# Decay attention and two feed-forward stages on one core: blocks rebuilt at an even pace, weight casts spaced out, sums kept in PSUM, and a minimum by a one-tensor operation

## The chip, the core and the metric

The kernel runs on one core of a Trainium2 chip. The metric is the device time of one execution in microseconds (us), the median of three runs. One execution was also profiled; all rows below come from it.

## What is computed

```python
scores = (q @ k^T) / 8 + (cum[i] - cum[j])      # cum = cumsum(log(clip(f, 1e-4, 1))), causal
attn = softmax(scores);  x = attn @ v           # 4 batches, 8 heads, 576 rows, 64 columns
h = x @ w_in;   x = (h * clip(h + 3, 0, 6) / 6) @ w_out       # 2304 tokens, 512 -> 2048 -> 512
h = x @ w_in2;  out = (max(h, 0) + alpha * min(h, 0)) @ w_out2  # alpha per column of h
```

Inputs are fp32; the weights come as 64-bit floats that the kernel itself turns into fp32. Every fp32 product is made of three fp32r products: high by high, high by low, low by high.

## The kernel before

The whole program is one hand-written order of instructions for each engine (a manual schedule); nothing reorders it later.

**Attention** works on 16 pairs of heads, 9 units a pair: four blocks of 128 rows of head a, a tail unit with the last 64 rows of both heads, four blocks of head b. A unit passes through stages that lag one another by a few units: PE makes scores (L364 to L381), DVE row maxima (`maxes`, L341; the tail unit has two columns of maxima, whose smaller one L343 keeps, both negated), ACT the exponentials with row sums (L349), PE the transposes (L397), ACT or DVE their copies (L408, L413). Per pair follow the reciprocals of the row sums (`recips`, L420 to L424), the product with v (L454) and its scaling into `r` (L461). `prep_head` and `prep_low` split the q and k of one head into high and low parts (POOL L92, POOL L332, DVE L333); two rows of sums of logarithms ride along as extra rows of k, taken from DRAM scratch `aq_d` and `ak_d` (L313, L314). The program's beginning builds these rows: `ak` on DVE, `aq` on POOL, then DMAs to scratch.

**Side work** stands in tables of name and unit. `CONV_ATT` gives the unit at which each step of the conversion of the first weights is issued: `m`, `f`, `s`, `j`, `g` turn raw words into fp32 (ACT L137, DVE L140, L144, L148, L153), `S1` to `S4` add or subtract weight blocks (POOL L167), `h` and `l` cast to high and take the low part (ACT L181, POOL L185). `fetch` loads raw weights. `CONV_TURN` is such a table for the start of the second feed-forward stage, in slots after the set at which it is started.

**The feed-forward stages** are 48 sets (stage, group of 256 columns of h, block of 768 tokens). A set has seven products (`product`, L700, six matmuls each) that form four blocks of h from seven sums of blocks, in PSUM banks hA (two), hB and hC. Between the products stand the pieces of the set before: L731 in the first stage, L733 in the second, which multiply by w_out. After a product, `keep` copies it (ACT L705) or `add` adds it to a kept copy (DVE L708), and `activate` follows: L663 (first stage) or L666 and L668 (second) on ACT, then DVE L674 or L677, then ACT's high copy L682 and POOL's low part L683, which the pieces need. The queue `later` sets what must follow, `aside` puts side work behind it in the slot. `build` rebuilds the input blocks of the next token block: 8 adds (L237), 14 casts to high (ACT L240), 14 low parts (L245). For two of them the places come from `BUILD`, for others from `BUILD_FIRST` at an even rate.

Of the kernel before, what the change touches and what calls it, by code (L numbers as in the profile page):

```python
# [21 lines left out]
def decay_attention_ffn2_kernel(ctx, tc, qk, v, f, wi1, wo1, wi2, wo2, alpha, out):  # L22
    nc = tc.nc
# [22 lines left out]
    CONV_ATT = "m0 15 f0 16 s0 17 j0 18 g0 19 m1 24 f1 25 s1 26 j1 27 g1 28 hb 33 lb 35 S1 42 S3 42 S2 44 S4 44 ha 51 la 53 hc 53 lc 60 hd 60 ld 62 m2 69 f2 70 s2 71 j2 72 g2 73 m3 78 f3 79 s3 80 j3 81 g3 82 ho0 78 lo0 80 ho1 87 lo1 89 wi0 90 wi1 93 wo0 99 wo1 102"  # L46
# [231 lines left out]
    def attention():  # L278
        with ExitStack() as ax:
# [57 lines left out]
            def maxes(parts, dsts):  # L337
# [4 lines left out]
                if n == 2:  # L342
                    nc.vector.tensor_tensor(out=nm[:, 0:1], in0=nm[:, 0:1], in1=nm[:, 1:2], op=ALU.min)  # L343
# [153 lines left out]
            nc.sync.dma_start(out=alpha_sb, in_=alpha)  # L497
            aug_consts(0)
# [5 lines left out]
            nc.gpsimd.memset(aq.bitcast(F32)[:, :, 512:640], 0.0)  # L504
            nc.gpsimd.memset(aq.bitcast(F32)[:, 2:4, 0:512], -1.0)
# [44 lines left out]
            aside(2, lambda: fetch(0), lambda: fetch(1))  # L550
# [103 lines left out]
    def activate(s, gt, i, n, h, d):  # L654
# [5 lines left out]
        def first():  # L660
# [28 lines left out]
    def product(s, c, gt, k):  # L689
# [17 lines left out]
        def add(k2):  # L707
            nc.vector.tensor_add(out=c[k2], in0=h, in1=c[k2])  # L708
# [194 lines left out]
```

## Time and profile before

| quantity | value |
|---|---|
| runs | 1013.59, 1015.56, 1016.53 us; median 1015.56 |
| profiled execution | 1012.13 us, of which the span of the instructions is 1010.3 |
| mean granted clock of PE | 0.995 of full speed |
| PE busy | 965.5 us, 96% of the span |
| DVE busy | 735.9 us, 73% |
| ACT busy | 589.1 us, 58% |
| POOL busy | 590.0 us, 58% |
| bytes moved by DMA | 147.57 MB |

An engine is busy in the time of its computing instructions. PE is TensorE, DVE VectorE, ACT ScalarE, POOL GpSimd, SP the engine whose queue issues most DMAs. In a timeline, the brackets at a row's end give the idle time ahead of it and what ended it.

### The profile page before, as it was taken

What the parts mean: (1) busy time and instruction counts of PE and PEld (TensorE: products, weight loads), DVE (VectorE), ACT (ScalarE), POOL (GpSimd) and SP (SyncE); (2) the same over time, 40 slices, a digit from 0 to 9 for tenths busy, and PEclk for the clock granted to TensorE, in tenths of its full rate; (3) what the DMA queues carried; (4) which work ended last, traced back from release to release, by engine and by line L of the source; (5) the groups of instructions that cost most, each with busy time, mean ns of one, the idle gap of its engine ahead of it and who ended that gap; (6) DMA issues with size and microseconds to landing.
All of it is one profiled execution on the core that took longest, in us unless ns stands there. A gap on an engine that the chain in (4) does not pass through costs nothing.

```text
span 1010.3 us, 15919 instructions
## 1 busy us (share of the span) xinstructions
PE 965.5 (96%) x5488; PEld 859.7 (85%) x5488; DVE 735.9 (73%) x1284; ACT 589.1 (58%) x1444; POOL 590.0 (58%) x577
## 2 busy tenths in 40 slices
PE   4999999999999999999999989999999999999998
PEld 3767666678899999998998988789898888898997
DVE  6888988857698788878989846145687788735454
ACT  5677787776555555555654445665565656564452
POOL 8567568956646666566485269566556556532222
PEclk9999999999999999999999999999999999999999
DMA  6555576501424444310576851332344420243531
GB/s 219 174 173 168 176 239 208 150 2 42 156 66 177 178 175 169 107 48 1 198 308 241 308 184 48 137 129 81 125 160 168 166 84 1 104 182 142 229 150 68
DMA packets 36868, 147.57 MB, mean 146 GB/s; under 512 B 4668, under 2 KB 4668, under 8 KB 33652
## 3 DMA queue, kind: packets, MB, share of 16 engines
q1 hardware_dynamic: 36784, 146.56, 41.7%
q8 instruction: 43, 0.70, 0.3%
q14 instruction: 37, 0.30, 0.1%
q10 hardware_dynamic: 4, 0.00, 0.0%
HBM read 98.26 MB, written 44.14 MB: 141 GB/s over the span
## 4 chain that ended last, share of the span: by engine, by line
PE 57%; DVE 23%; POOL 7%; ACT 6%; issue 4%; DMA 2%; SPq 0%; POOLq 0%; ACTq 0%; DVEq 0%
PE o L733 13%; PE hA L700 12%; PE o L731 12%; PE hC L700 7%; PE pv L454 4%; PE hB L700 3%; DVE nm L341 3%; PE tp L397 2%; DVE t L674 2%; PE sc L364 2%; POOL wi L185 2%; POOL g L683 1%; DVE r L751 1%; DVE s L708 1%; ACT g L682 1%
## 5 line engine op out<-in xcount | busy, mean ns | idle before, releaser
L731 PE MATMUL o<-g,wo 128*128 128x384 f32 x1152 | 233.3, 341 | 2.0 <-POOL g L683 2.0
L700 PE MATMUL hA<-xh,wi 128*128 128x384 f32 x768 | 225.8, 339 | 9.0 <-ACT s L705 5.4
L733 PE MATMUL o<-wo,g 128*128 128x512 f32 x864 | 225.5, 395 | 4.0 <-POOL g L683 3.0
L683 POOL TENSOR_TENSOR g<-t,g 128x384 fp32r<-128x384 f32 x120 | 128.8, 1073 | 156.1 <-ACT g L682 134.6
L731 PEld LDWEIGHTS o<-g,wo 128*128 128x128 f32 x1152 | 205.6, 189 | 4.6 <-POOL g L683 3.3
L733 PEld LDWEIGHTS o<-wo,g 128*128 128x128 f32 x864 | 159.8, 188 | 33.2 <-POOL g L683 6.2
L683 POOL TENSOR_TENSOR g<-s,g 128x384 fp32r<-128x384 f32 x72 | 74.7, 1038 | 155.6 <-ACT g L682 153.8
L700 PEld LDWEIGHTS hA<-xh,wi 128*128 128x128 f32 x768 | 142.0, 188 | 15.1 <-ACT s L705 7.6
L751 DVE TENSOR_TENSOR r<-o,r 128x512 f32<-128x512 f32 x126 | 86.2, 687 | 73.8 <-PE o L733 73.7
L700 PE MATMUL hA<-xl,wi 128*128 128x384 f32 x384 | 129.7, 338 | 0.0
L682 ACT CAST g<-t 128x384 fp32r<-128x384 f32 x120 | 61.9, 515 | 113.0 <-DVE t L674 97.3
L700 PE MATMUL hC<-xh,wi 128*128 128x384 f32 x384 | 115.0, 340 | 3.6 <-ACT s L705 3.6
L740 DVE SCALAR_TENSOR_TENSOR r<-o,r 128x384 f32<-128x384 f32 x168 | 90.6, 549 | 21.2 <-PE o L731 21.0
L349 ACT ACTIVATE p<-sc,nm 128x128 f32<-128x128 f32 (+4 forms) x160 | 84.6, 532 | 22.9 <-DVE nm L341 10.9
L245 POOL TENSOR_TENSOR xl<-r,xh 128x384 fp32r<-128x384 f32 x65 | 78.5, 1225 | 4.1 <-ACT xh L240 3.7
L341 DVE TENSOR_REDUCE nm<-sc 128x1 f32<-128x128 f32 (+4 forms) x160 | 71.7, 470 | 10.1 <-PE sc L366 8.5
L700 PEld LDWEIGHTS hC<-xh,wi 128*128 128x128 f32 x384 | 71.3, 189 | 6.7 <-ACT s L705 4.6
L700 PEld LDWEIGHTS hA<-xl,wi 128*128 128x128 f32 x384 | 72.4, 189 | 3.1
L682 ACT CAST g<-s 128x384 fp32r<-128x384 f32 x72 | 37.1, 515 | 60.1 <-DVE s L677 53.4
L397 PE MATMUL tp<-ident,p 128*128 128x128 f32 x384 | 68.6, 282 | 0.6 <-ACT pt L413 0.6
L364 PE MATMUL sc<-k,q 128*128 128x256 f32 (+2 forms) x128 | 55.6, 434 | 11.9 <-DVE k L332 9.8
L700 PE MATMUL hC<-xl,wi 128*128 128x384 f32 x192 | 65.1, 339 | 0.0
(128 smaller groups left out, 1901.8 us busy)
## 6 DMA issues: line engine op xcount, KB each, us to landing
wid<-wi SPq DMA_DIRECT2D x24, 896.0 KB
wi<-wid SPq DMA_DIRECT2D x12, 1792.0 KB
rqk<-in_qk SPq DMA_DIRECT2D x32, 608.0 KB
raw<-in_wi SPq DMA_DIRECT2D x32, 512.0 KB
raw<-in_wo SPq DMA_DIRECT2D x32, 512.0 KB
wod<-wo SPq DMA_DIRECT2D x24, 512.0 KB
wo<-wod SPq DMA_DIRECT2D x12, 1024.0 KB
vt<-in_v SPq DMA_DIRECT2D x16, 320.0 KB
```

What stands on the lines that cost most here:

```text
L245: e.tensor_sub(out=XS[k][1][:, b, c], in0=x, in1=XS[k][0][:, b, c].bitcast(F32))
L341: nc.vector.tensor_reduce(out=nm[:, i:i + 1], in_=src, axis=AX.X, op=ALU.max, negate=True)
L349: nc.scalar.activation(out=pt[:, c0:c0 + cw], in_=src, func=AF.Exp, bias=nm[:, 0:1], scale=1.0, accum_out=dsts[i])
L364: nc.tensor.matmul(out=sc[:, 0:n], lhsT=q1[:, qs], rhs=k1[:, 0:n], start=True, stop=False)
L397: nc.tensor.transpose(tp[:, j, :], pt[:, 128 * j:128 * j + 128], ident)
L682: nc.scalar.copy(out=gt[n][i][:, 0], in_=hold["g"])
L683: nc.gpsimd.tensor_sub(out=gt[n][i][:, 1], in0=hold["g"], in1=gt[n][i][:, 0].bitcast(F32))
L700: nc.tensor.matmul(out=h, lhsT=a, rhs=b[:, x, kc], start=new and kc + e == 0, stop=kc == KH - 1 and e == 2, skip_group_check=not new)
L731: nc.tensor.matmul(out=o[:, 0:NB], lhsT=a[:, cs], rhs=b, start=st, stop=sp)
L733: nc.tensor.matmul(out=o, lhsT=b[:, cs], rhs=a, start=st, stop=sp)
L740: later(0, lambda: nc.vector.scalar_tensor_tensor(out=acc, in0=o[:, 0:NB], scalar=1.0 / 6.0, in1=acc, op0=ALU.mult, op1=ALU.add))
L751: nc.vector.tensor_add(out=acc, in0=o, in1=acc)
```

## The change

It has seven parts. (1) The minimum L343 becomes a tensor_scalar with the second column as the scalar. (2) The scratch rows `aq_d` are written by DMA straight from `ak` and from constants, without POOL's copies; the preparation of head 1 moves behind the masks on POOL. (3) The first two raw weight loads and the conversions that use them move to later units. (4) `CONV_TURN` gets other slots. (5) All rebuilds take their places from one list, at an even rate that depends on the rebuild; in two of them the eight adds move from DVE to POOL and the low parts are shared out evenly. (6) `add` leaves its sum in the PSUM bank, except for product 7. (7) The second stage's activation is written as h + (1 - alpha) * relu(-h), without the second Relu.

```diff
-    CONV_ATT = "m0 15 f0 16 s0 17 j0 18 g0 19 m1 24 f1 25 s1 26 j1 27 g1 28 hb 33 lb 35 S1 42 S3 42 S2 44 S4 44 ha 51 la 53 hc 53 lc 60 hd 60 ld 62 m2 69 f2 70 s2 71 j2 72 g2 73 m3 78 f3 79 s3 80 j3 81 g3 82 ho0 78 lo0 80 ho1 87 lo1 89 wi0 90 wi1 93 wo0 99 wo1 102"
+    CONV_ATT = "m0 20 f0 21 s0 22 j0 23 g0 24 m1 26 f1 27 s1 28 j1 29 g1 30 hb 34 lb 35 S1 42 S3 42 S2 44 S4 44 ha 51 la 53 hc 53 lc 60 hd 60 ld 62 m2 69 f2 70 s2 71 j2 72 g2 73 m3 78 f3 79 s3 80 j3 81 g3 82 ho0 78 lo0 80 ho1 87 lo1 89 wi0 90 wi1 93 wo0 99 wo1 102"
...
-    CONV_TURN = "p0 0 p1 0 S1 6 S2 7 S3 7 hc 8 ha 8 lc 9 hb 9 la 10 lb 11 S4 12 hd 13 ld 14 p2 14 p3 15 ho0 24 lo0 25 ho1 26 lo1 27 wi0 40 wi1 43 wo0 46 wo1 48"
-    BUILD_FIRST = "h0 l0 a3 h3 l3 h2 l2 a4 a6 h6 l6 h4 l4 h1 l1 a5 h5 l5"
-    BUILD = "h0 2 l0 4 a3 6 h3 9 l3 11 h2 9 l2 11 a4 13 a6 15 h4 16 l4 18 h1 17 l1 19 h6 19 l6 21 a5 22 h5 26 l5 28"
+    CONV_TURN = "p0 0 p1 0 S1 5 S2 6 S3 7 hc 9.5 ha 10.5 lc 10.6 la 11.5 hb 12 lb 13 S4 14 hd 17 ld 18 p2 15 p3 18.5 ho0 24 lo0 25 ho1 26 lo1 27 wi0 40 wi1 43 wo0 46 wo1 48"
+    BUILD_FIRST = "h0 l0 a3 a4 h3 h2 l2 l3 a6 h4 l4 h1 h6 l1 a5 l6 h5 l5"
...
-    def build_ops(k, p, add, subs, even=None):
+    def build_ops(k, p, add, subs, even):
         adds, highs, lows = build_parts(k, p, add, subs)
-        if even is not None:
...
-        return [(t, {"h": highs, "l": lows, "a": adds}[name[0]][int(name[1]), c])
-                for name, t in table(BUILD) for c in range(KH)]
+        fns = [{"h": highs, "l": lows, "a": adds}[name[0]][int(name[1]), c]
+               for name in BUILD_FIRST.split() for c in range(KH)]
+        return [(even[0] + i / even[1], fn) for i, fn in enumerate(fns)]
...
                 if n == 2:
-                    nc.vector.tensor_tensor(out=nm[:, 0:1], in0=nm[:, 0:1], in1=nm[:, 1:2], op=ALU.min)
+                    nc.vector.tensor_scalar(out=nm[:, 0:1], in0=nm[:, 0:1], scalar1=nm[:, 1:2], scalar2=None, op0=ALU.min)
...
-            aq = pro.tile([NPP, 4, QW], F32R, name="aq")
+            aq = pro.tile([NPP, 2, QW], F32, name="aq")
...
+            nc.gpsimd.memset(aq, -1.0)
+            for a in range(2):
+                nc.gpsimd.memset(aq[32 * a:32 * a + 32, :, 576 - 64 * a:640 - 64 * a], 0.0)
...
             nc.sync.dma_start(out=alpha_sb, in_=alpha)
+            nc.sync.dma_start(out=aq_d.rearrange("a h r c -> (a h) r c")[:, 2:4], in_=aq)
+            for a in range(2):
+                nc.sync.dma_start(out=aq_d[a, :, 0:2, 576 - 64 * a:640 - 64 * a],
+                                  in_=zero[32 * a:32 * a + 32, 0:128].rearrange("p (r c) -> p r c", r=2))
...
             load_head(2)
+            nc.sync.dma_start(out=aq_d.rearrange("a h r c -> (a h) r c")[:, 0:2, 0:512], in_=hl[:, :, 0:512].bitcast(F32))
+            for a in range(2):
+                ps, t0 = slice(32 * a, 32 * a + 32), 512 + 64 * a
+                nc.sync.dma_start(out=aq_d[a, :, 0:2, t0:t0 + TAIL], in_=hl[ps, :, 512:S].bitcast(F32))
             for a in range(2):
                 nc.sync.dma_start(out=ak_d[a, 0:NP], in_=ak[32 * a:32 * a + NP].bitcast(F32))
             load_head(3)
-            prep_head(1)
-            prep_low(1)
...
-            scaled("P", aq[:, 0:2, 0:512], hl[:, :, 0:512].bitcast(F32))
-            for a in range(2):
-                ps, t0 = slice(32 * a, 32 * a + 32), 512 + 64 * a
-                scaled("P", aq[ps, 0:2, t0:t0 + TAIL], hl[ps, :, 512:S].bitcast(F32))
-            for a in range(2):
-                nc.sync.dma_start(out=aq_d[a, 0:NP], in_=aq[32 * a:32 * a + NP].bitcast(F32))
-            nc.gpsimd.tensor_scalar(out=alpha_sb, in0=alpha_sb, scalar1=-1.0, scalar2=None, op0=ALU.mult)
+            prep_head(1)
+            prep_low(1)
+            nc.gpsimd.tensor_scalar(out=alpha_sb, in0=alpha_sb, scalar1=-1.0, scalar2=1.0, op0=ALU.mult, op1=ALU.add)
...
-            aside(2, lambda: fetch(0), lambda: fetch(1))
+            aside(13, lambda: fetch(0))
+            aside(18, lambda: fetch(1))
...
             nc.scalar.activation(out=t, in_=h(), func=AF.Relu, scale=-1.0)
-            hold["g"] = g32 = P["tp"].tile([128, NB], F32, tag="t", name="t") if (i, n) == (1, 0) else h()
-            nc.scalar.activation(out=g32, in_=h(), func=AF.Relu)
-            hold["t"] = t
+            hold["g"] = t
...
-                nc.vector.scalar_tensor_tensor(out=g32, in0=hold["t"], scalar=alpha_sb[:, m:m + 1], in1=g32,
+                nc.vector.scalar_tensor_tensor(out=g32, in0=g32, scalar=alpha_sb[:, m:m + 1], in1=h(),
                                                op0=ALU.mult, op1=ALU.add)
...
         def add(k2):
-            nc.vector.tensor_add(out=c[k2], in0=h, in1=c[k2])
+            got = h if k != 7 else c[k2]
+            nc.vector.tensor_add(out=got, in0=h, in1=c[k2])
+            c[k2] = got
...
-                build(0, 1, (nc.gpsimd, nc.vector), nc.gpsimd)
+                build(0, 1, (nc.gpsimd, nc.vector), nc.gpsimd, (1, 1.35))
         if (g, p) == (NG - 1, 0):
-            build(1 if ff else 0, 2, both)
+            build(1 if ff else 0, 2, (nc.vector, nc.gpsimd), nc.gpsimd, (1, 1.5 if ff else 1.3))
```

The order of PE's instructions is the same before and after. Three places on other engines follow.

POOL at the program's beginning, before (aq and ak are the rows of sums, k_176 the k of head 1, ident, maskj and three constants):

```order
L506 MEMSET ak 64x1152
L92 TENSOR_SCALAR k_169<-rqk 128x576
L516 MEMSET aq 32x2x64 x2
L92 TENSOR_SCALAR k_176<-rqk 128x576
L332 TENSOR_TENSOR k_176<-rqk,k_176 64x576
L524 MEMSET three 128x1
masks.py:197 MEMSET ident 128x128
masks.py:199 AFFINE_SELECT ident<-ident 128x128
L526 MEMSET maskj 128x64
L528 AFFINE_SELECT maskj<-maskj 64x64 x2
L92 TENSOR_SCALAR aq<-ak 64x2x512
L92 TENSOR_SCALAR aq<-ak 32x2x64 x2
```

The same place with the change:

```order
L507 MEMSET ak 64x1152
L91 TENSOR_SCALAR k_175<-rqk 128x576
L525 MEMSET three 128x1
masks.py:197 MEMSET ident 128x128
masks.py:199 AFFINE_SELECT ident<-ident 128x128
L527 MEMSET maskj 128x64
L529 AFFINE_SELECT maskj<-maskj 64x64 x2
L91 TENSOR_SCALAR k_182<-rqk 128x576
L328 TENSOR_TENSOR k_182<-rqk,k_182 64x576
L534 TENSOR_SCALAR alpha_sb<-alpha_sb 128x16
```

The three copies into aq are gone, and the two instructions that prepare head 1 stand behind the masks.

DVE in the third pair of attention, from the end of a conversion to the tail's minimum, before (nm are row maxima, rc the reciprocals, wb the weights being converted):

```order
L153 SCALAR_TENSOR_TENSOR wb<-raw,wb 128x512
L341 TENSOR_REDUCE nm<-sc 128x1
L420 TENSOR_SCALAR sm<-sm 128x1
L422 COPY sm<-sm 128x1
L423 TENSOR_SCALAR rc<-sm 128x10
L424 RECIPROCAL rc<-rc 128x10
L341 TENSOR_REDUCE nm<-sc 128x1 x2
L408 COPY pt<-tp 128x4x128
L341 TENSOR_REDUCE nm<-sc 128x1 x2
L343 TENSOR_TENSOR nm<-nm 128x1
L333 SCALAR_TENSOR_TENSOR q_846<-rqk,q_845 64x640
```

The same place with the change, where the lines have other numbers (L416 to L420 are the reciprocals, L337 the reductions, L339 the minimum, L147 and L152 the last steps of the conversion):

```order
L416 TENSOR_SCALAR sm<-sm 128x1
L418 COPY sm<-sm 128x1
L419 TENSOR_SCALAR rc<-sm 128x10
L420 RECIPROCAL rc<-rc 128x10
L147 SCALAR_TENSOR_TENSOR wb<-raw,wb 128x512
L337 TENSOR_REDUCE nm<-sc 128x1
L152 SCALAR_TENSOR_TENSOR wb<-raw,wb 128x512
L337 TENSOR_REDUCE nm<-sc 128x1
L404 COPY pt<-tp 128x4x128
L337 TENSOR_REDUCE nm<-sc 128x1 x2
L339 TENSOR_SCALAR nm<-nm 128x1
L329 SCALAR_TENSOR_TENSOR q_843<-rqk,q_842 64x640
```

The two last steps of the conversion stand behind the reciprocals instead of ahead of them.

ACT at the start of the second feed-forward stage, around the kept copies L705, before (wi are the weights being cast, r the output sum):

```order
L181 CAST wi<-wc 128x2x256
L181 CAST wi<-wa 128x2x256
L682 CAST g_7703<-t 128x384
L181 CAST wi<-wb 128x2x256
L705 COPY s<-hA 128x384
L749 COPY r_80<-o 128x512
L705 COPY s<-hC 128x384
L749 COPY r_80<-o 128x512
L181 CAST wi<-wb 128x2x128
L705 COPY s<-hA 128x384
```

The same place with the change (L701 is the kept copy, L180 the cast, L747 the copy to the output sum):

```order
L180 CAST wi<-wc 128x2x256
L701 COPY s<-hA 128x384
L180 CAST wi<-wa 128x2x256
L747 COPY r_80<-o 128x512
L701 COPY s<-hC 128x384
L180 CAST wi<-wb 128x2x256
L747 COPY r_80<-o 128x512
L701 COPY s<-hA 128x384
L747 COPY r_80<-o 128x512
L664 ACTIVATE t<-hC 128x384
L747 COPY r_80<-o 128x512
L180 CAST wi<-wb 128x2x128
```

Of the four casts to wi three stood ahead of the first kept copy and one ahead of the third; now one stands ahead of the first, one ahead of the second, one ahead of the third, and the last behind all of them.

## Rows read from the trace of the kernel before

**Rows 1.** The page's part 4, the chain that ended last, by engine.
```profile
PE 57%; DVE 23%; POOL 7%; ACT 6%; issue 4%; DMA 2%; SPq 0%; POOLq 0%; ACTq 0%; DVEq 0%
```

**Rows 2.** Six stretches: length; busy us of PE, PEld, DVE, ACT, POOL; PEclk; DMA share, GB/s.
```profile
25.00:50.00 25.00, 24.50 (x177) 17.41 (x178) 19.88 (x46) 17.62 (x62) 12.38 (x14) 0.93 0.55 178
...
225.00:250.00 25.00, 22.90 (x125) 21.93 (x122) 19.43 (x27) 15.42 (x34) 13.82 (x13) 0.93 0.13 43
...
450.00:475.00 25.00, 22.75 (x127) 21.85 (x127) 21.50 (x36) 13.15 (x28) 14.10 (x12) 1.00 0.01 4
...
575.00:600.00 25.00, 22.35 (x124) 22.03 (x123) 13.26 (x25) 10.54 (x21) 11.08 (x11) 0.98 0.67 241
...
625.00:650.00 25.00, 21.26 (x104) 18.29 (x104) 7.71 (x13) 17.16 (x37) 18.23 (x19) 1.00 0.36 136
...
850.00:875.00 25.00, 22.92 (x110) 19.49 (x109) 20.78 (x31) 15.39 (x34) 15.03 (x13) 1.00 0.17 64
```

**Rows 3.** Timeline of PE: start, us, line, operation, tiles, shape [idle before <-releaser].
```profile
11.66 0.55 PE L365 MATMUL sc<-k,q 68*128 68x256 f32 x1 [1.34 <-DVE q L333]
...
25.06 0.35 PE L365 MATMUL sc<-k,q 68*128 68x256 f32 x1 [3.86 <-DMA k<-ak_d]
...
59.30 0.45 PE L364 MATMUL sc<-k,q 128*128 128x384 f32 x1 [0.30 <-ACT p L349]
...
60.37 2.42 PE L454 MATMUL pv<-pt,vt 128*64 128x320 f32 x20
...
463.26 0.44 PE L700 MATMUL hA<-xh,wi 128*128 128x384 f32 x1 [1.62 <-ACT s L705]
```

**Rows 4.** The chain in order of time, start of the run: start, us, what.
```profile
14.56 5.79 DMA aq_d<-aq
...
20.73 4.20 DMA k<-ak_d
```

**Rows 5.** Timeline of POOL, attention.
```profile
15.72 0.73 POOL L92 TENSOR_SCALAR q<-rqk 128x640 fp32r<-128x640 f32 x1 [0.48 <-DMA rqk<-in_qk]
...
57.14 1.41 POOL L332 TENSOR_TENSOR k<-rqk,k 64x576 fp32r<-64x576 f32 x1
...
150.60 1.89 POOL L332 TENSOR_TENSOR k<-rqk,k 64x576 fp32r<-64x576 f32 x1
```

**Rows 6.** The answer on line L343 (ns minimum/median/maximum, first and last start).
```profile
L343 DVE TENSOR_TENSOR nm<-nm x16: 159/1372/1385, 17.6 to 206.8; 128x1 f32<-128x1 f32 x16
...
  ACT p L349: 9.7, 12
```

**Rows 7.** The answer on line L420, columns as in 6.
```profile
L420 DVE TENSOR_SCALAR sm<-sm x16: 193/196/206, 26.7 to 213.4; 128x1 f32<-128x1 f32 x16
```

**Rows 8.** Timeline of DVE, attention and the set at 455.
```profile
43.80 1.38 DVE L343 TENSOR_TENSOR nm<-nm 128x1 f32<-128x1 f32 x1
...
57.18 1.38 DVE L343 TENSOR_TENSOR nm<-nm 128x1 f32<-128x1 f32 x1
...
59.42 0.41 DVE L461 TENSOR_TENSOR r<-pv,rcb 128x256 f32<-128x256 f32 x1
...
69.10 1.38 DVE L343 TENSOR_TENSOR nm<-nm 128x1 f32<-128x1 f32 x1
...
76.09 1.54 DVE L333 SCALAR_TENSOR_TENSOR q<-rqk,q 64x640 fp32r<-64x640 f32 x1
...
151.66 0.20 DVE L420 TENSOR_SCALAR sm<-sm 128x1 f32<-128x1 f32 x1
...
459.09 2.67 DVE L237 TENSOR_TENSOR r<-r 128x384 f32<-128x384 f32 x2
```

**Rows 9.** The answer on line L674, those with a PSUM bank.
```profile
L674 DVE SCALAR_TENSOR_TENSOR t<-t,hA x24: 542/554/556, 230.0 to 612.0; 128x384 f32<-128x384 f32 x24
```

**Rows 10.** The answer on line L237, those of POOL.
```profile
L237 POOL TENSOR_TENSOR r<-r x24: 995/1198/1542, 160.4 to 625.6; 128x384 f32<-128x384 f32 x24
```

**Rows 11.** Timeline of ACT in the set at 630.
```profile
639.08 0.40 ACT L181 CAST wi<-wb 128x256 fp32r<-128x256 f32 x1 [4.16 <-POOL wb L167]
```

More of the change, by code (lines that the diff above doesn't have):

```diff
@@ L255, in build_parts @@
         return adds, highs, lows
-    def build_ops(k, p, add, subs, even=None):
+    def build_ops(k, p, add, subs, even):
         adds, highs, lows = build_parts(k, p, add, subs)
-        if even is not None:
-            fns = [{"h": highs, "l": lows, "a": adds}[name[0]][int(name[1]), c]
-                   for name in BUILD_FIRST.split() for c in range(KH)]
-            return [(even[0] + i / even[1], fn) for i, fn in enumerate(fns)]
-        return [(t, {"h": highs, "l": lows, "a": adds}[name[0]][int(name[1]), c])
-                for name, t in table(BUILD) for c in range(KH)]
+        fns = [{"h": highs, "l": lows, "a": adds}[name[0]][int(name[1]), c]
+               for name in BUILD_FIRST.split() for c in range(KH)]
+        return [(even[0] + i / even[1], fn) for i, fn in enumerate(fns)]
     def x_places(c, t0, t1):
@@ L503, in attention @@
                                     fill=-1.0e9, base=0, channel_multiplier=1)
-            nc.gpsimd.memset(aq.bitcast(F32)[:, :, 512:640], 0.0)
-            nc.gpsimd.memset(aq.bitcast(F32)[:, 2:4, 0:512], -1.0)
             nc.gpsimd.memset(ak[:, 0:2, :].bitcast(F32), 1.0)
@@ L514, in attention @@
             prep_low(0)
-            for a in range(2):
-                nc.gpsimd.memset(aq.bitcast(F32)[32 * a:32 * a + 32, 2:4, 512 + 64 * a:576 + 64 * a], -1.0)
             aug_rows(1)
             load_head(2)
+            nc.sync.dma_start(out=aq_d.rearrange("a h r c -> (a h) r c")[:, 0:2, 0:512], in_=hl[:, :, 0:512].bitcast(F32))
+            for a in range(2):
+                ps, t0 = slice(32 * a, 32 * a + 32), 512 + 64 * a
+                nc.sync.dma_start(out=aq_d[a, :, 0:2, t0:t0 + TAIL], in_=hl[ps, :, 512:S].bitcast(F32))
             for a in range(2):
@@ L530, in attention @@
                                         fill=-1.0e9, base=0, channel_multiplier=1)
-            scaled("P", aq[:, 0:2, 0:512], hl[:, :, 0:512].bitcast(F32))
-            for a in range(2):
-                ps, t0 = slice(32 * a, 32 * a + 32), 512 + 64 * a
-                scaled("P", aq[ps, 0:2, t0:t0 + TAIL], hl[ps, :, 512:S].bitcast(F32))
-            for a in range(2):
-                nc.sync.dma_start(out=aq_d[a, 0:NP], in_=aq[32 * a:32 * a + NP].bitcast(F32))
-            nc.gpsimd.tensor_scalar(out=alpha_sb, in0=alpha_sb, scalar1=-1.0, scalar2=None, op0=ALU.mult)
+            prep_head(1)
+            prep_low(1)
+            nc.gpsimd.tensor_scalar(out=alpha_sb, in0=alpha_sb, scalar1=-1.0, scalar2=1.0, op0=ALU.mult, op1=ALU.add)
             px.close()
@@ L764, in conversion, with build @@
                     aside(t * scale + shift, ops[name])
-        def build(k, pair, subs, add=nc.vector, even=None):
+        def build(k, pair, subs, add=nc.vector, even=(1, 1.5)):
             for t, fn in build_ops(k, pair, add, subs, even):
@@ L772, in side_work @@
             conversion(early["first"], CONV_FIRST, True)
-            build(1, 1, both, even=(1, 1.5))
+            build(1, 1, both)
         if s == (0, 0, 1):
```

## The prediction

> **What bounds the kernel now.** I read the page first: its list of engines (the table above: PE busy 96% of the span, DVE 73%, ACT and POOL 58%), then its chain, which is PE for 57% and DVE for 23% [rows 1]. So no engine has to become faster. A change pays where PE stands idle, or where the chain runs through DVE. Then the table by stretches of 25 us [rows 2]: the reader is to see how much of 25 us PE lacks in each, and the granted clock. In attention (to about 215 us) PE and DVE are both nearly full and feed each other. In the two feed-forward stages a few stretches lack more than others: 2.25 at 450, 2.65 at 575, 3.74 at 625, 2.08 at 850. They hold rebuilds of input blocks and conversions of weights, which the change reorders. Last I read PE's own timeline for the stalls behind these numbers and what released each [rows 3].
>
> The clock: the stretches at 25 and at 225 read 0.93, at 450 it reads 1.00 [rows 2]. The first lies right behind a stall of 3.86 us, the one at 450 holds one of 1.62 us [rows 3]. Clock of 0.93 over 25 us is 25 x 0.07 = 1.75 us of full clock that was not given (part of the time at the lower of the two levels, 1.2 GHz). So the long stall costs its length and 1.75 us more, the short one its length only.
>
> **The change part by part**
>
> *Start.* Once begun, PE stops for 1.34 us until DVE's L333 has made q, and again for 3.86 us at 25.06, released by the DMA into k [rows 3]. The chain shows why: aq_d is written from 14.56 and takes 5.79 us, then the DMA from scratch to k another 4.20 [rows 4]. Ahead of 14.56 stands POOL's step that makes aq. The change drops it: the scratch rows come from ak, which DVE finishes before the L333 that PE waits for until 11.66, so their writes can start up to 2.9 us earlier. The two raw weight loads (fetch, 512 KB each), issued between the two DMAs of that chain, go to units 13 and 18. Four DMAs more stand in SP's queue: the three with constants where SP still waits for ak, one more with rows ahead of the DMA into k; I price these at nothing, with half a us each as the worst. POOL's L332 of head 1, which runs beside the L333 in question, goes behind the masks, as the order of POOL shows; that gives at most the 1.34. Upper bound: 1.34 + 3.86 + 1.75 = 6.95. Against it: POOL can begin head 2 only when its load has landed, at 15.72 [rows 5], which the change leaves as it is; and L332 of head 1 now meets DVE's second L333. Lower bound 3.5, the write 1.75 us earlier and the clock kept. I take **-5.5**, nearer the top, because the path gains 2.9 us and no longer shares its time with 1 MB of weights.
>
> *The minimum (L343).* A comparison of 128 single numbers takes 159 ns at best and 1372 in the median; ACT waits 9.7 us for it, in 12 of 16 pairs [rows 6]. At 57.18 it takes 1.38 and so ends at the end of POOL's L332, which runs from 57.14 for 1.41 [rows 5, 8]. The new form (one tensor, the other column as scalar) has a twin here, L420: 193 to 206 ns in all 16 [rows 7]. One of them, at 151.66 with 0.20, lies inside a POOL L332 from 150.60 to 152.49 [rows 5, 8]. So I price it at 0.20. What is late next: L333 comes right behind and reads two SBUF tensors. At 76.09 it took 1.54 beside an L332 [rows 8], which will be its fate more often. DVE as a whole thus gains nothing, but the tail's exponentials start 1.38 - 0.20 = 1.18 us earlier. PE waits for them 0.30 us at 59.30 [rows 3], and its next pv product needs DVE's L461, which starts at 59.42, behind L333, and takes 0.41 [rows 8]. That product started at 60.37 [rows 3], so it can move forward by some 0.5 us until it meets L461's end at 59.83. Ten pairs of the 12 at that price: **-5**. Bounds: 0 (all of it moves to L333) and 12 x 1.18 = 14.2. I take what the worked pair gives.
>
> The Trainium skill speaks against this part: "SBUF — State Buffer", section "Who interferes with whom", says that a tensor_scalar can enter a mode that uses both ports, and that such an instruction and one of GpSimd then block each other for their whole length. By it the new form could wait as the old did, and this term would be 0. L420's 0.20 beside L332 disagrees, for one element per partition; rival 3 is this.
>
> *Conversion of the first weights* moves from units 15-19 and 24-28 to 20-24 and 26-30. The pair from 43.80 to 57.18, with one conversion, takes 13.38; the next, to 69.10 and without, 11.92 [rows 8]: 1.46 a conversion. The new place lies in DVE's burst of work between the reductions and L343, shown in the order of DVE, where nothing covers it, since ACT and PE wait for that burst's end. I take half as much again for the two, **+1.5**; bounds -1 (less work in the pair that starts the two loads) and +3, both paid once more.
>
> *Sums in place, one Relu less.* 96 instructions of ACT go; ACT is no bound, but the chain from sum to product (L708, L666, L668, L677, L682, L683) loses a step. The sums of banks B and C stay in PSUM. DVE's second step with a PSUM bank as second tensor, L674, takes 542 to 556 ns in all 24 [rows 9], never stretched, so it costs nothing to read there. No row shows DVE writing PSUM. I take the same 0.55, with 0.45 and 0.8 as bounds: 96 x 0.25 = 24 us of DVE work at worst, beside PE work, since DVE has 27% of its time free.
>
> *Stalls of the feed-forward stages, place by place.* At 463.26 PE waits 1.62 us for ACT's copy L705 [rows 3]; it stands behind L682, which needs DVE, which is in two L237 from 459.09, 2.67 us together [rows 8]. The eight L237 of this rebuild go to POOL, and some two L245 come back. POOL has 14.10 busy of 25 there [rows 2], and 8 x 1.20 [rows 10] less 2 x 1.2 makes about 21: **-2** of the 2.25, bounds -3 and +2 (POOL's L683 late instead). At 575-600 PE lacks 2.65; there L705 stands behind an L181 that waits for POOL's L167 and that for weights from DRAM, and in the new order one such L181 still precedes it: **0**. At 625-650 PE lacks 3.74; in it, at 639.08, an L181 that had waited 4.16 us for POOL stands ahead of an L705 [rows 11]. In the new order of ACT that L181 stands behind the L705, and those ahead of the two others are moved in the same way: **-3** of the 3.74 of that stretch, bounds -5 and +1. At 850-875, where the second stage's rebuild meets the long chain through ACT, PE lacks 2.08 [rows 2]: **-2**, bounds -3 and +2, by the same exchange of L237 (POOL 15.03 busy) and the Relu less. At 225-250 PE lacks 2.10 [rows 2]; nothing that stands ahead there is removed, but L674 and L677 read PSUM instead of a second SBUF tensor there and in the fuller stretches: **-1.6**, an estimate between 0 and 3. Sum: -8.6.
>
> **Sum.** -5.5 - 5 + 1.5 - 8.6 = -17.6. The profiled execution has a span of 1010.3 and a time of 1012.13; the span would be 992.7 and its time 994.5. The median shown, 1015.56, lies 3.4 above that execution, so I predict **998.0 us**.
>
> **The rivals**
> 1. *It only moves the waits.* L343's gain goes to L333 (for it: 1.54 at 76.09; against: PE's direct wait at 59.30), and half of the stalls in the feed-forward stages stay. -5.5 + 0 + 1.5 - 4.3 = -8.3: 1007.3.
> 2. *More than that.* The tail's wait is worth its full 1.18 us in ten pairs (against it: L461 at 59.42), the conversions cost nothing in their new place, and the feed-forward stages give 12. -5.5 - 11.8 - 12 = -29.3: 986.3.
> 3. *The new form waits like the old* for the port that L332 holds, by whatever form it has. Then the rest alone: -12.6, 1003.0. L420 speaks against.
> 4. *The start gains little*, because the load of head 2 is last and not the scratch rows (POOL starts at 15.72, released by the landing). Start -1.1 instead of -5.5: 1002.4. Against: PE's stall is ended by the DMA into k, not by POOL.
> 5. *Slower: POOL becomes the bound in the two rebuilds*, in the sets about 455 and 855 us, where 8 adds of 1.2 us each go to POOL, for whose L683 every output product waits. If each add stands ahead of an L683 that PE needs, a rebuild costs 9.6 us and one clock drop of 1.75, twice 11.3 = 22.7; the two gains of 2 us there go as well. -17.6 + 4 + 22.7 = +9.1: 1024.7. It decides once POOL has no free time left in its 25 us; by the sum above it has about 21 busy.
>
> **How the numbers follow.** About 0.3% (3 us) is what a measurement of this kernel tells from no change. Chances: forecast 0.42, rival 1 0.18, rival 2 0.12, rival 3 0.10, rival 4 0.09, rival 5 0.09. The first five are all faster; since their bad terms can meet, I count 0.05 of their 0.91 as no change, and 0.02 of rival 5 (POOL late in one rebuild only) as well: faster 0.86, same 0.07, slower 0.07. The range of 986 to 1010 us leaves out rival 5, half of rival 2 and a little of rival 1, in all 0.18.
>
> **What would show it.** Right: L339 (the old L343) at 0.2 us with the L329 behind it at up to 1.5; no stall over 1 us for k<-ak_d, and a granted clock of 1.00 in 25-50; PE above 24 in the stretches at 450, 625 and 850; a stall near 598 that is still there; the in-place sum (L705, the old L708) at about 0.55. Wrong: POOL at 25 of 25 us in a rebuild while PE waits for L679 (the old L683); the sum in PSUM above 1 us; pairs of attention that still take 12 to 13 us.

## The result and the profile after

The changed kernel takes 998.13 us in the median (998.00 to 1001.61, 4 runs) against 1014.58 (1012.88 to 1016.53, 4 runs of the kernel before): a ratio of 0.9846, interval 0.9816 to 0.9875. The prediction was 998.0. That is nearer than its working deserves. The profiled executions are 1012.13 and 998.00 us, 14.1 apart where the sum said 17.6. The prediction then added the 3.4 us by which the median of before lay above its profiled execution; the changed kernel's own offset is 0.1. The two errors cancel, and the parts show where the first comes from (times of DVE's minimum, whose starts number the pairs of attention, and of PE's matmuls):

| stretch | before | after | difference | forecast |
|---|---|---|---|---|
| to the minimum of the second pair | 31.10 | 28.20 | -2.9 | -5.5 |
| from there to the minimum of the sixth pair | 50.27 | 52.84 | +2.6 | +1.5, less what L343 gives in four pairs |
| from there to the second set | 145.81 | 143.58 | -2.2 | what L343 gives in the other pairs (in all -5) |
| second set to the last matmul | 779.35 | 767.66 | -11.7 | -8.6 |

These are two single executions. In four other kernels below whose attention is the same code as the change's, the first three rows read 27.75 to 29.20, 50.61 to 53.21 and 143.33 to 146.11. So the first difference is clear of chance only in its sign (-1.9 to -3.4), the second lies between +0.3 and +2.9, and the third is not clear of chance at all.

The page's busy times and chain, after:

```profile
PE 960.9 (96%) x5488; PEld 862.8 (87%) x5488; DVE 711.8 (71%) x1274; ACT 540.6 (54%) x1348; POOL 590.8 (59%) x583
...
PE 80%; DVE 7%; POOL 4%; issue 3%; DMA 3%; ACT 2%; SPq 1%; POOLq 0%; ACTq 0%; DVEq 0%
```

DVE's share of the chain falls from 23% [rows 1] to 7%. Stretches of 25 us of the changed kernel, columns as in [rows 2]:

```profile
25.00:50.00 25.00, 24.95 (x197) 18.20 (x196) 21.71 (x52) 19.77 (x72) 14.73 (x16) 1.00 0.63 198
50.00:75.00 25.00, 21.71 (x154) 15.55 (x154) 16.88 (x36) 15.00 (x54) 15.67 (x18) 0.86 0.55 162
225.00:250.00 25.00, 22.92 (x126) 21.55 (x124) 19.13 (x29) 17.62 (x40) 16.51 (x15) 1.00 0.13 43
250.00:275.00 25.00, 22.16 (x117) 21.84 (x118) 14.56 (x26) 12.63 (x27) 15.25 (x16) 0.93 0.43 158
450.00:475.00 25.00, 25.00 (x144) 25.00 (x143) 19.32 (x34) 13.58 (x29) 20.14 (x19) 1.00 0.00 1
575.00:600.00 25.00, 22.18 (x125) 21.53 (x124) 10.71 (x21) 10.93 (x23) 15.22 (x16) 1.00 0.45 164
600.00:625.00 25.00, 23.01 (x118) 21.99 (x117) 18.59 (x27) 13.76 (x31) 24.81 (x24) 0.93 0.32 116
625.00:650.00 25.00, 25.00 (x125) 22.47 (x124) 7.05 (x11) 16.29 (x33) 13.86 (x14) 1.00 0.40 148
850.00:875.00 25.00, 25.00 (x126) 22.55 (x125) 15.61 (x27) 9.66 (x21) 11.29 (x12) 1.00 0.31 112
```

The stretches at 450, 625 and 850, which lacked 2.25, 3.74 and 2.08 us [rows 2], lack nothing now. (The changed kernel is up to 13 us ahead by then, so the stretches hold somewhat different work; the sets, further down, say the same.) Three lack more than they did: 3.29 at 50, 2.84 at 250 and 1.99 at 600, where the same stretches of the kernel before lacked 0.89, 1.88 and 0.85:

```profile
50.00:75.00 25.00, 24.11 (x183) 16.91 (x182) 21.04 (x45) 18.14 (x67) 15.86 (x19) 1.00 0.60 175
250.00:275.00 25.00, 23.12 (x129) 22.19 (x129) 16.94 (x28) 14.67 (x32) 17.03 (x17) 1.00 0.42 158
600.00:625.00 25.00, 24.15 (x130) 23.51 (x130) 16.45 (x27) 13.87 (x30) 22.71 (x22) 0.96 0.16 54
```

PE's timeline names the stalls there and at the start, with what released them (against [rows 3]):

```profile
10.08 0.55 PE L361 MATMUL sc<-k,q 68*128 68x256 f32 x1 [0.68 <-ACT q L87]
...
19.92 0.45 PE L360 MATMUL sc<-k,q 128*128 128x384 f32 x1 [2.01 <-ACT p L345]
...
53.42 0.58 PE L374 MATMUL sc<-k,q 68*128 68x288 f32 x1 [3.29 <-DMA k<-k]
...
251.95 0.45 PE L696 MATMUL hA<-xl,wi 128*128 128x384 f32 x1 [2.36 <-POOL xl L244]
...
591.93 0.44 PE L696 MATMUL hC<-xh,wi 128*128 128x384 f32 x1 [2.57 <-ACT s L701]
...
603.74 0.62 PE L729 MATMUL o<-g,wo 128*128 128x384 f32 x2 [1.52 <-ACT g L678]
```

The 3.86 us for k<-ak_d are gone; 2.01 at 19.92 stand in their place. ACT's timeline shows whose wait that is:

```profile
19.11 0.27 ACT L404 COPY pt<-tp 128x128 f32<-128x128 f32 x1 [4.16 <-DMA q<-aq_d]
19.27 0.51 ACT L345 ACTIVATE p<-sc,nm 128x288 f32<-128x288 f32 x1
```

ACT's first copy into pt waits 4.16 us, with the exponentials queued behind it. The row names one DMA; the chain leads from this copy to the write ak_d<-ak, issued at 14.02 (12.24 before) behind the new scratch writes and landed at 18.78. The code opens the pool of pt where the pool of ak is closed, so pt most likely reuses ak's memory and waits until ak has been read; that was not tried by itself. The clock behind the 2.01 us reads 0.78, 0.50 and 0.86 in windows of 2 us from 20 on, so a drop as before is paid here too. It fits the account that in all eight kernels with the new scratch rows ACT stands idle 2.78 to 4.16 us ahead of this copy, and 0.99 to 1.62 us in the six with the old ones. What it costs PE differs with the DMAs: in a2 and a7, with the same attention code, no stall over 0.8 us stands at 20 us, but one of 1.58 and 1.82 us for the first rows of k at 11.

### The profile page after: what moved, and what is told of

The parts are those of the page before. It is cut to its first block, busy times and chain, and to the rows that moved or that the text cites. A ratio compares the mean times of both kernels' runs of the same rounds, so it can differ in the third digit from the quotient of the medians.

```text
span 995.9 us, 15848 instructions
## 1 busy us (share of the span) xinstructions
PE 960.9 (96%) x5488; PEld 862.8 (87%) x5488; DVE 711.8 (71%) x1274; ACT 540.6 (54%) x1348; POOL 590.8 (59%) x583
## 4 chain that ended last, share of the span: by engine, by line
PE 80%; DVE 7%; POOL 4%; issue 3%; DMA 3%; ACT 2%; SPq 1%; POOLq 0%; ACTq 0%; DVEq 0%
PE o L731 19%; PE hA L696 17%; PE o L729 15%; PE hC L696 9%; PE pv L450 5%; PE hB L696 4%; PE tp L393 4%; PE sc L360 2%; PE sc L361 2%; DMA k<-k 1%; POOL g L679 1%; DVE t L670 1%; PE sc L362 1%; DMA fd<-wa 1%; PE sc L374 1%
## 5 line engine op out<-in xcount | busy, mean ns | idle before, releaser
L679 POOL TENSOR_TENSOR g<-t,g 128x384 fp32r<-128x384 f32 x192 | 202.6, 1056 | 286.8 <-ACT g L678 269.0
L678 ACT CAST g<-t 128x384 fp32r<-128x384 f32 x192 | 98.7, 514 | 189.4 <-DVE t L673 93.1
L345 ACT ACTIVATE p<-sc,nm 128x128 f32<-128x128 f32 (+4 forms) x160 | 84.1, 528 | 14.1 <-DVE nm L337 12.4
L337 DVE TENSOR_REDUCE nm<-sc 128x1 f32<-128x128 f32 (+4 forms) x160 | 71.3, 468 | 10.5 <-PE sc L362 6.6
L244 POOL TENSOR_TENSOR xl<-r,xh 128x384 fp32r<-128x384 f32 x59 | 68.3, 1170 | 4.2 <-ACT xh L239 4.0
L701 ACT COPY s<-hA 128x384 f32<-128x384 f32 x96 | 45.8, 477 | 37.2 <-PE hA L696 36.9
L696 PE MATMUL hB<-xh,wi 128*128 128x384 f32 x192 | 57.1, 338 | 0.0
```

The lines of the kernel that those rows point to most:

```text
L244: e.tensor_sub(out=XS[k][1][:, b, c], in0=x, in1=XS[k][0][:, b, c].bitcast(F32))
L337: nc.vector.tensor_reduce(out=nm[:, i:i + 1], in_=src, axis=AX.X, op=ALU.max, negate=True)
L345: nc.scalar.activation(out=pt[:, c0:c0 + cw], in_=src, func=AF.Exp, bias=nm[:, 0:1], scale=1.0, accum_out=dsts[i])
L678: nc.scalar.copy(out=gt[n][i][:, 0], in_=hold["g"])
L679: nc.gpsimd.tensor_sub(out=gt[n][i][:, 1], in0=hold["g"], in1=gt[n][i][:, 0].bitcast(F32))
L696: nc.tensor.matmul(out=h, lhsT=a, rhs=b[:, x, kc], start=new and kc + e == 0, stop=kc == KH - 1 and e == 2, skip_group_check=not new)
```

## The experiments

Eleven of the twelve kernels undo one part of the change, or make one part alone, or put parts together that looked better; the last one moves casts further. In the changed kernel and all built on it, attention differs from run to run with the DMAs: the second set begins between 222.04 and 227.61 in five kernels whose attention is the same code (the change, a2, a5, a6, a7). So parts of the feed-forward stages are judged by the time from the second set's first matmul to the last matmul ("feed-forward time"), and parts of attention by the starts of DVE's minimum. The feed-forward code was the same, too, in the change, a1, a3 and a4: 767.39 to 770.10, which is the noise there. Nearly all of it lies in the third set and in the three sets at the turn of the stages (the 24th to the 26th, together 54.0 to 55.9 us in kernels with the change's code there); the other sets repeat within 0.1 us in most cases, so they can be compared one by one. No kernel takes back the even places of the rebuilds alone; what they give is only what the other parts leave over. Each ratio below is to runs of the kernel before that were made beside that kernel, so it is not the quotient of two medians of the table.

| kernel | median us | ratio to before (interval) | feed-forward time us |
|---|---|---|---|
| before | 1014.58 | 1 | 779.35 |
| minimum alone | 1011.96 | 0.9978 (0.9968 to 0.9988) | 779.86 |
| raw loads later alone | 1012.16 | 0.9979 (0.9969 to 0.9989) | 779.88 |
| the change | 998.13 | 0.9846 (0.9816 to 0.9875) | 767.66 |
| a1, minimum back | 1001.32 | 0.9881 (0.9861 to 0.9902) | 767.39 |
| a2, l6 early | 995.99 | 0.9823 (0.9799 to 0.9846) | 765.89 |
| a3, conversion back | 995.90 | 0.9822 (0.9805 to 0.9839) | 768.49 |
| a4, start back | 996.89 | 0.9837 (0.9815 to 0.9858) | 770.10 |
| a5, adds back | 1001.94 | 0.9879 (0.9857 to 0.9900) | 770.31 |
| a6, sums back | 1004.64 | 0.9892 (0.9866 to 0.9917) | 776.55 |
| a7, turn back | 1000.96 | 0.9870 (0.9849 to 0.9891) | 770.21 |
| c1, a2 and a3 | 993.59 | 0.9791 (0.9776 to 0.9806) | 765.67 |
| c2, a2, a3 and a4 | 995.39 | 0.9808 (0.9789 to 0.9827) | 766.19 |
| c3, c2 and casts later | 992.15 | 0.9781 (0.9764 to 0.9798) | 763.59 |

**The minimum: undone in the change (a1), and alone in the kernel before.**

```diff
-  nc.vector.tensor_scalar(out=nm[:, 0:1], in0=nm[:, 0:1], scalar1=nm[:, 1:2], scalar2=None, op0=ALU.min)
+  nc.vector.tensor_tensor(out=nm[:, 0:1], in0=nm[:, 0:1], in1=nm[:, 1:2], op=ALU.min)
```

> The change with the old two-tensor minimum. Theory of the prediction (about 0.5 us in each of ten pairs): 5 us slower than the change, 1003. Rival A, read from the changed trace (undisturbed pairs run only 0.2 us shorter than before, the old L333 behind it now 1.14 us in the median instead of 0.81): about 2.3 us slower, 1000.4. Rival B, the whole wait moved to the next instruction: no difference, 998. The median of the minimum should be 1.37 us again and that of the next instruction 0.81.

> The kernel before with the new minimum alone. Theory of the prediction: 5 us faster than before. Theory after the first runs (from the start of the sixth pair's minimum to the sixteenth's 123.3 us with the new form and 124.7 with the old one, on the changed kernel): 1.5 to 2.5 us faster over 16 pairs. Rival: nothing (within 0.5 us), since the wait only moves to the next instruction. In the trace the minimum takes 0.21 us, and ten pairs together are 1 to 2 us shorter (or 5, or not).

The answers on the two lines, L339 and L329 in the changed kernel and L333 in the kernel before:

```profile
L339 DVE TENSOR_SCALAR nm<-nm x16: 212/214/216, 16.0 to 204.4; 128x1 f32<-128x1 f32 x16
...
L329 DVE SCALAR_TENSOR_TENSOR q<-rqk,q x32: 806/1138/1916, 8.7 to 199.0; 64x640 fp32r<-64x640 f32 x32
```
```profile
L333 DVE SCALAR_TENSOR_TENSOR q<-rqk,q x32: 804/808/2011, 9.7 to 201.9; 64x640 fp32r<-64x640 f32 x32
```

The minimum takes 0.21 us in all 16 against 1.37 in the median [rows 6], and the next instruction goes from 0.81 to 1.14: the wait moved, as foretold; in a1 they are 1.37 and 0.81 again. What is left is smaller than foretold. The proof is the kernel with the minimum alone: it gives 2.2 us in twelve runs (the interval allows 1.2 to 3.2), so 0.08 to 0.20 a pair, not 0.5. The pairs of one execution can't settle it: from the sixth pair to the sixteenth it is 123.32 us in the change and 124.73 in a1, but 122.87 to 125.76 in the five kernels with the change's attention. The medians of a1 and the change differ by 3.2, and their intervals overlap.

**The start (a4, and the raw loads alone).** a4 takes the start of the kernel before; the other moves only the fetches in the kernel before.

```diff
-            aside(2, lambda: fetch(0), lambda: fetch(1))
+            aside(8, lambda: fetch(0))
+            aside(10, lambda: fetch(1))
```

> The change with the old building of the scratch rows (aq made by POOL, two DMAs from it, head 1 prepared ahead of the masks); the raw loads stay at units 13 and 18. Theory of the prediction: the rows are what is last, 5.5 us in all, so 1002 to 1003.6 (the lower end if the raw loads alone already shorten the DMAs). Rival, from the changed trace (the second and third pair begin 2.9 and 3.1 us earlier than before, a new stall of 2.01 us at 19.92 for the exponentials): 3 us, 1001. If the raw loads were all of it: 998.

> The kernel before with nothing but its first two raw weight loads moved, from unit 2 to units 8 and 10. Theory after the first runs (with the old scratch rows and the loads moved, the second pair's minimum came at 27.30 instead of 31.10): the loads are the whole gain of the start. Then the stall of 3.86 us for k<-ak_d falls below 1 us, and the time by 3 to 5 us against before. Theory of the prediction: both are needed, so 1 to 2 us here. Rival: no gain, another load takes their place in the queue.

Chain and PE of the kernel with the loads alone moved:

```profile
14.55 6.07 DMA aq_d<-aq
...
21.02 1.56 DMA k<-ak_d
```
```profile
22.72 0.36 PE L365 MATMUL sc<-k,q 68*128 68x256 f32 x1 [0.79 <-DMA k<-ak_d]
```

The write from POOL's aq still takes 6 us, but the DMA back into k takes 1.56 instead of 4.20 [rows 4], the stall 0.79 instead of 3.86, and the second pair's minimum comes at 27.30. In a4, with the loads at 13 and 18, it is 27.30 as well; in the change, with new rows too, 28.20. So the raw loads were the first stall, not the scratch rows. All executions bear this out: the second pair's minimum comes at 31.10 and 32.45 with the old rows and the old loads, at 26.84 to 27.83 with the old rows and the loads moved (four kernels), at 27.75 to 29.39 with both changed (eight). And a4's median of 996.89 is not above the change's, where the prediction's theory asked for 1002 to 1003.6. But the load is only moved: with the loads alone the gain is down to 1.5 us at the third pair (42.27 against 43.80 [rows 8]) and 0.6 at the fifth (68.50 against 69.10). By its ten runs the kernel with the loads alone gains 2.0 us (interval 1.1 to 3.1), less than the 3 to 5 that were expected of it.

**The conversion of the first weights (a3).**

```diff
-    CONV_ATT = "m0 20 f0 21 s0 22 j0 23 g0 24 m1 26 f1 27 s1 28 j1 29 g1 30 hb 34 lb 35
+    CONV_ATT = "m0 15 f0 16 s0 17 j0 18 g0 19 m1 24 f1 25 s1 26 j1 27 g1 28 hb 33 lb 35
...
-            aside(13, lambda: fetch(0))
-            aside(18, lambda: fetch(1))
+            aside(8, lambda: fetch(0))
+            aside(10, lambda: fetch(1))
```

> The change with the first two conversions back at units 15-19 and 24-28 (casts of b at 33), and the two raw loads at units 8 and 10, behind the loads of heads 2 to 4. Theory: the stall of 3.29 us at 53.42 for the copy of k, with the lower clock behind it, comes from the raw load that the moved conversion triggers at unit 24, right ahead of that copy; without it the time falls by 3 to 5 us, to 993 to 995. The prediction's theory (conversion in the burst costs 1.5 us by DVE work): 996.5. Rival: the two raw loads early in the run delay the rows of k for head 2 and a stall of 1 to 4 us comes back near 20 to 25 us: 998 to 1002.

The queue of SP ahead of the stall at 53.42, and the chain there, in the change:

```profile
43.67 0.36 SPq L116 DMA_DIRECT2D raw<-in_wo  x1
...
44.79 0.36 SPq L291 DMA_DIRECT2D rqk<-in_qk  x1
45.53 0.36 SPq L296 DMA_DIRECT2D vt<-in_v  x1
45.98 0.47 SPq L322 DMA_DIRECT2D k<-k  x1
```
```profile
45.98 7.30 DMA k<-k
```

The step `sign` fetches the next raw weights. At its new unit that load (512 KB) goes out within 2.3 us of rqk and vt and ahead of the copy k<-k, which PE needs; the copy takes 7.30 us. In a3 no PE stall over 0.3 us stands there, and the sixth pair's minimum comes at 78.12 instead of 81.04. The stall is no chance: at this place PE waits 2.31 to 3.90 us in all seven kernels with the change's units for these conversions (in a4 the profile names DVE for it), and at most 0.3 us in all four that have the old units and the raw loads at 8 and 10 (a3, c1, c2, c3). Its price is less certain: in the four other kernels with the change's attention code the sixth pair comes at 78.36 to 82.29, and the median of a3 is 2.2 us lower with intervals that overlap. a3 moves conversions and raw loads together, and no run parts the two. The clock behind the stall reads 0.50 in three windows of 2 us in the change (52 to 58); behind the 2.40 us of a1 it stays at 1.00.

**The first rebuild (a2).** All rebuilds use the change's new list; here the first one has h6 and l6 earlier.

```diff
-"h0 l0 a3 a4 h3 h2 l2 l3 a6 h4 l4 h1 h6 l1 a5 l6 h5 l5"
+"h0 l0 a3 a4 h3 h2 l2 l3 a6 h4 h6 l6 l4 h1 l1 a5 h5 l5"
```

> The change, but in the first rebuild the blocks h6 and l6 stand four places earlier in the list; nothing else moves. Theory: the set at 241 us takes 22.64 us instead of 15.77 because PE's product 6 waits 2.36 us for the low part l6, issued in the same slot, and the clock drops behind it. Then this set takes 16 to 19 us and the time falls by 3 to 6 us, to 992 to 995. Rival: the waits of the set come from DVE being full of old adds and conversions; then the wait moves to l4 or l1 and the time stays within 1.5 us of 998.

The stall of 2.36 us for xl, 10.7 us into the third set, is gone, and the next one, 18.6 us into it, is 1.58 us for ACT's high copy of g. The third set takes 19.7 us instead of 22.6 (22.6 to 23.9 in all kernels with the change's list here), the fourth 1 us more. So the order in the list is shown to cost about 2 us. Theory and rival are each half right: the set is faster, but over 19 us, and the median falls by 2.1, with intervals that overlap.

**The rebuilds' adds (a5), the sums in PSUM with one Relu less (a6), the turn (a7).**

```diff
-            build(1 if ff else 0, 2, (nc.vector, nc.gpsimd), nc.gpsimd, (1, 1.5 if ff else 1.3))
+            build(1 if ff else 0, 2, both, nc.vector, (1, 1.5 if ff else 1.3))
```
```diff
-            got = h if k != 7 else c[k2]
-            nc.vector.tensor_add(out=got, in0=h, in1=c[k2])
-            c[k2] = got
+            nc.vector.tensor_add(out=c[k2], in0=h, in1=c[k2])
```

In a6 the activation's lines and the sign of alpha are those of before as well; a7 has the old `CONV_TURN`.

> The change with the eight adds of the rebuilds at about 450 and 850 us on DVE again and the low parts two on POOL to one on DVE; places at the new even rate. Theory of the prediction: DVE's adds ahead of the activation are what made PE wait there, 2 us each: 4 us slower than the change, 1002; the 16th set again at 18 us or more. Rival A: the even places alone do it, the adds could be on either engine: 998. Rival B: POOL was the worse place: faster, 996.

> The change with the sums of all products in SBUF again and the second Relu back (the old activation whole). Theory: the chain through ACT and the two-input reads beside POOL cost the sets of the second stage at 788, 820, 853 and 870 us (by the two traces 0.7, 0.7, 1.4 and 1.5) and the second set of the first stage 3.05: 3 to 7 us slower than the change, 1001 to 1005. Rival: those gains come from the even rebuilds, and the shorter chain is worth under 1 us.

> The change with the old slots of the conversion at the turn of the stages. Theory of the prediction: the casts ahead of the kept copies cost what the set at 625 us lost, 4.5 us by the two traces, of which 2.7 came back in the set ahead of it: 2 to 4.5 us slower, 1000 to 1002.5, with stalls over 1 us for kept copies at about 620 to 630. Rival: the loss only goes from one set to its neighbour, since POOL has the same work there in either order: 998.

The stretch with the second stage's rebuild, in the change, in a5 and in a6:

```profile
835.00:860.00 25.00, 24.94 (x124) 22.12 (x123) 19.38 (x31) 14.30 (x33) 22.55 (x21) 1.00 0.17 64
```
```profile
835.00:860.00 25.00, 23.49 (x114) 19.99 (x113) 22.24 (x33) 11.04 (x25) 14.17 (x13) 1.00 0.11 42
```
```profile
835.00:860.00 25.00, 23.58 (x115) 20.42 (x114) 20.86 (x29) 15.65 (x36) 23.06 (x20) 1.00 0.09 32
```

PE lacks 1.5 us there with the adds on DVE and 1.4 with the long chain, 0.06 with neither. In this rebuild the 40th set takes 17.95 us in a5, 17.74 in a6 and 16.09 in the change, against 17.44 before: the adds are worth about 2 us here, as the prediction's theory had it. In the first stage's rebuild they matter little: the 16th set takes 16.1 us in a5, 16.4 in a6 and 15.84 in the change, against 18.81 before. What is left of its gain, and the 1.5 us of the 41st set, which is the same in a5, a6 and the change, fall to the even places; that is argued from what is left over, not shown. a6 is the largest part that was undone: 8.9 us more feed-forward time than the change, spread over ten sets, while the noise is 2.7. Some 3.6 of it lie ahead of the turn, where the activations are alike and only the sums differ, and 4.0 behind it, where sums and Relu were not parted. Of the sets that were named for a6, those at 788, 820 and 853 lose 0.7, 0.7 and 1.7, about as expected, the one at 870 nothing, and the second set 0.4, not 3.05. a7 is 2.6 us more, which that noise does not settle; the set at 625 loses 2.7 us with the old slots (a stall of 1.50 us for a kept copy stands in it at 630.16) and nothing to 1.0 with the new ones, but the three sets of the turn together take 56.2 us against 54.0 to 55.9.

**Together (c1, c2, c3).**

> The change with h6 and l6 early in the first rebuild and the first two conversions back at their old units, with their raw loads at units 8 and 10. If the two gains add (2.1 and 2.2 us by the medians): 994, with no stall for k<-k near 53 us and a set at about 240 us of 20 us or less. Rival: part of either was chance of the DMAs, 996 to 998.

> The one before, and the old building of the scratch rows. If the old rows cost nothing once the raw loads are away, or are the better ones (the median with them was 1.2 us lower): 992.5 to 994. Rival: raw loads at units 8 and 10, nearer the beginning than 13 and 18, meet the later scratch DMAs: a stall of 1 to 3 us at 20 to 26 us, 996.

> The one before, and the sums and casts of the conversion at the turn three slots later, so that the first kept copy of bank C stands ahead of all casts. Theory: the 2.3 to 3.5 us of stall at about 590 us and the clock drop behind it go: 3 to 5 us faster than without, 988 to 991. Rival: POOL, busy in all of 590 to 608 us in the changed kernel, only meets the low parts later, and the set after takes what this one gains: no difference.

c1 is faster than both kernels: 993.59 us (992.80 to 993.94), ratio 0.9791 (0.9776 to 0.9806), below the change's interval. As expected, it has no stall for k<-k near 53 us, and its third set takes 19.7 us. Its profile has a mean granted clock of 1.000. Stretches:

```profile
25.00:50.00 25.00, 24.59 (x190) 17.45 (x189) 22.67 (x47) 18.81 (x69) 13.01 (x15) 1.00 0.60 193
50.00:75.00 25.00, 24.62 (x190) 17.68 (x189) 21.32 (x49) 19.09 (x73) 17.62 (x19) 1.00 0.64 190
```

c2 hints that the old scratch rows cost something once the raw loads come early: in c1 SP is done with the first rows for k at 17.84, in c2 at 20.81, and the loads and the next rqk follow later; the third pair's minimum is at 42.94 instead of 40.66. With the same start as c2 it is 41.52 in c3, and with the same as c1 41.57 in a3, and the intervals of c1 and c2 overlap, so this is not shown. In c3 the step S4 runs ahead of the cast of block b, which it should follow, so one block of weights has other values and the output is not that of the reference; kinds and number of instructions are the same. So its time is no offer of a faster kernel and tells only of the order. It gains 2.6 us of feed-forward time over c2, but not by ending the stall: that is 3.48 us at 595.08 now, for DVE's sum, behind ACT's cast L181, which waits 4.60 us for POOL's L167. The stall moves with POOL's queue: the rival had the mechanism nearer. In time the median is 3.2 us lower, with intervals that overlap.

## Why the prediction was right

- *The bound and the kind of gain*: right. PE's busy time hardly changes (965.5 to 960.9), its gaps do.
- *Start, -5.5*: measured -2.9 (-1.9 to -3.4 with the other kernels of the same attention code). **The step that failed** is "the path gains 2.9 us and no longer shares its time with 1 MB of weights": only its second half was the cause, as a4 and the loads alone show, and the new writes put ak_d's write later, behind which ACT and then PE wait (2.01 us with its own clock drop in this execution). The size lies between the forecast and rival 4's -1.1, whose reason was another.
- *Minimum, -5*: measured -2.2 alone (-1.2 to -3.2). The mechanism was right (0.21 us, wait handed to the next instruction), the term was mis-sized: half a us was read from one pair behind a conversion, and the mean over 16 pairs is 0.14. One sign of being wrong came: of the 14 steps from one pair's minimum to the next, from the second pair on, eight still take over 12 us, as before. Rival 3, that the new form waits like the old, is refuted: 212 to 216 ns in all 16, of which 14 lie inside a POOL TENSOR_TENSOR.
- *Conversion, +1.5*: +2.4 to +2.9 between a3 and the change (at the second set and at the sixth pair), but anything from +0.2 to +4.2 with the other kernels of the change's attention code. The price was taken from DVE's work; what the runs show is a DMA stall, from a load that the moved step triggers. That every DMA of a moved step counts was not followed up to `sign`.
- *Sums in place*: right in price (below), but its worth was put inside other terms; a6 makes it the largest part.
- *Feed-forward stages, -8.6*: measured -11.7. The 16th set gave 3.0 (forecast 2), of which the adds are about 0.3 (a5). The sets from 582 to 637 gave 2.9 (forecast 3): the stall for L701 stays, 2.57 us, as said, and the stalls of the set at 625 are gone. The second stage's rebuild gave 2.9 (forecast 2). The second to fourth sets lost 1.0 together (forecast a gain, 1.6 with the fuller stretches): the new list put l6 too late. The 20th to 22nd and the 34th to 39th sets gave 3.8 more, for which the sum has no place of its own; a6 loses most of it again, so it is mainly the sums and the Relu.
- *Rival 5*, POOL as the bound: not in the two rebuilds named (20.14 of 25 us at 450, foretold 21), but in the one at the turn. POOL has 24.81 of 25 us in the stretch at 600, and the set there, the 25th, lost 2.7 us. But in a1, a2, a3 and a5, with the same code at the turn and POOL as full, that set takes 16.1 to 17.3 us against 17.15 before, and the one ahead of it 20 to 22.4. So the wait goes to either set, and the place was missed.

## What to carry to other kernels

A load moved out of a full stretch lands in another: follow every DMA that the moved step triggers, and what stands behind it in the queue, before the move is priced. A wait taken from one instruction by a cheaper form goes to the next that needs the same resource, and what is left has to be read from several pairs, not from the best one. Where DMAs make one execution differ from the next, read the same wait in every kernel that has the same code there, before a difference of 1 or 2 us is given a cause. When a sum and a result agree, compare the terms: here a start, a minimum and a conversion were off by over 6 us together, and were covered by the feed-forward stages and by the offset of one profiled execution.

## What was not expected of the hardware

DVE writes its sum into PSUM as fast as into SBUF: 547 to 567 ns in place, 542 to 559 to SBUF. The activation's second step is often stretched with two SBUF tensors, and with a PSUM bank it is not:

```profile
L705 DVE TENSOR_TENSOR hB<-hB,s x48: 547/553/567, 216.2 to 981.5; 128x384 f32<-128x384 f32 x48
...
L705 DVE TENSOR_TENSOR s<-hA,s x48: 542/550/559, 221.2 to 979.1; 128x384 f32<-128x384 f32 x48
```
```profile
L670 DVE SCALAR_TENSOR_TENSOR t<-t,hC x24: 540/546/555, 222.5 to 597.7; 128x384 f32<-128x384 f32 x24
L670 DVE SCALAR_TENSOR_TENSOR t<-t,s x24: 543/932/1370, 224.1 to 601.8; 128x384 f32<-128x384 f32 x24
```

The Trainium skill, "SBUF — State Buffer", section "Who interferes with whom", says that a DVE instruction with two SBUF inputs contends with a GpSimd instruction that reads SBUF, and one with at most one such input outside the two-port modes does not. These rows agree: of the 24 with two SBUF tensors, the 14 over 0.6 us all ran beside a TENSOR_TENSOR of POOL, and of the 72 with a PSUM bank 43 did so too and none was over 0.56.

And the clock does not follow the length of a stall alone. Behind 2.01 us at 19.92 it fell to 0.50; behind 2.57 at 591.93 it stayed at 1.00, and in c1 behind 2.80 us at 587 as well, while before it fell behind 2.65 at 598. Even the same stall differs: behind 2.10 us at 243.26 the kernel before reads 0.50 (245 to 247), and the kernel with the loads alone moved reads 1.00 behind 2.10 us at 243.18. The prediction's "the long stall costs its length and 1.75 us more, the short one its length only" holds in some places only.
